# Two attention models in one kernel: both output products as Strassen's, from outputs kept in DRAM

## The chip, the cores and the metric

The kernel runs on one core of a Trainium2 chip. The metric is the device time of one execution in microseconds (us): the median of several runs. A core has five engines that run side by side, each with its own queue of instructions: TensorE (PE, matrix products into PSUM), VectorE (DVE), ScalarE (ACT), GpSimd (POOL) and SyncE (SP), which issues the DMA transfers here. An instruction waits at the head of its queue until the data and buffers it needs are ready, and what stands behind it waits too.

## The reference, cut to what matters

Two independent attention models over 2048 rows of 1024 columns; their outputs are put side by side. Both end in a product with a 1024x1024 matrix wo.

```python
def _A_ref(x, wq, wk, wv, wo, beta):      # 32 heads of 32, 4 segments of 512 rows
    q, k, v = heads(x @ wq), heads(x @ wk), heads(x @ wv)
    for s in range(4):
        p = softmax(q[s] @ k[s].T * scale + mask)
        o[s] = g * (phi(q[s]) @ M / (phi(q[s]) @ z + 1e-6)) + (1 - g) * (p @ v[s])
        M, z = M + phi(k[s]).T @ v[s], z + phi(k[s]).sum(rows)
    return o @ wo

def _B_ref(x, wqkv, w_phi, wo):           # 32 heads of 32
    q, k, v = split(x @ wqkv)
    phi_q = concat(softmax(q @ w_phi), softmax(-q @ w_phi))
    phi_k = concat(softmax(k @ w_phi), softmax(-k @ w_phi))
    kv, z = phi_k.T @ v, phi_k.sum(rows)
    return (phi_q @ kv / (phi_q @ z + 1e-6)) @ wo

return concatenate([A, B], axis=-1)
```

## The kernel before

**Number format.** TensorE multiplies 16-bit floats. Each 32-bit operand is scaled by a bound of its size and split into a high half (a rounded copy, ScalarE) and a low half (what is left, VectorE or GpSimd); one product of two such operands is three products of halves. `halves` records such a split. A product of 128 rows with a 1024x512 piece of weights is thus 8 x 3 = 24 matmuls of 512 columns, and a row block's whole output product 48.

**Strassen's product.** Where it is used, two blocks of 128 rows and the four quarters of the weights are combined into seven forms each, and seven half-depth products of 4 x 3 = 12 matmuls take the place of eight: 84 matmuls for two row blocks in place of 96. The forms of the rows cost four additions and seven splits, the outputs three additions out of PSUM.

**Stages.** First come the first model's attention (32 units of a segment and four heads), which leaves its outputs o in a DRAM tensor `oa_d`; in its course the second model's weights are prepared. Then, for each of eight pairs of row blocks, the second model's keys and values (Strassen's), their two softmaxes (`expo`) and the sums `kva`, `ez` and `za` over the rows. Then the second model's queries: for each of 16 row blocks its projection (Strassen's, by pairs, out of forms kept in `xf_d`), `expo`, multiplication with the sums of the keys (GpSimd), a split into halves `kls`, a transposing DMA into `pt`, and a small product with the sums into the bank `pv`, in two halves of 16 heads.

**The two output products.** The second model's (`project`) is plain: each half of a query block's result is split straight out of `pv` into a tile `ot` (ScalarE the high half, VectorE the low one), and 2 x 24 matmuls of it with wo (`bo`, prepared among the keys by `keep_bo` and kept in `bo_d`) follow within the queries, with one copy on ScalarE and a store for each half. The first model's stands last, as Strassen's: for each of eight pairs (row blocks c and c + 8) two loads from `oa_d`, four combinations (`comb`), seven splits, seven products (`mult`), four copies (`keep`) and three additions (`store`). Its weights are prepared among the queries (`sizes_out`, `weights`).

**What sets the order.** Every instruction is recorded with an engine, a duration, a priority and what it reads and writes (`Graph.op`), and a list scheduler (`Graph.run`) writes them out: at each step the engine that can start first takes, of those that can start then, the instruction with the lowest priority number. Numbers in the table NUDGE shift the priorities a little. PSUM has eight banks, given out by kind (`proj`, `s`, `misc`, `pv`, `kv`). Where the scheduler leaves TensorE without work for more than 0.5 us by its own reckoning and a bank is free, it puts a few matmuls into that bank which nobody reads (`fill`). Tiles with one tag share `bufs` buffers in turn, so an instruction that writes the next tile of a tag waits for the last reader of an earlier one.

Of the kernel before, what the change touches and what calls it, by code (L numbers as in the profile page):

```python
# [45 lines left out]
NUDGE = {0: 820989, 2: 102852, 3: 529656, 4: 266905, 5: 924189, 6: 435410, 9: 911235, 12: 450738, 13: 124130, 14: 669972,  # L46
# [59 lines left out]
class Graph:  # L106
# [12 lines left out]
    def __init__(self, pools):  # L119
        self.ops, self.tags, self.pools, self.opened, self.lines = [], {}, pools, {}, {}  # L120

# [21 lines left out]
    def op(self, eng, dur, fn, r=(), w=(), prio=0, lat=0.0, short=False, port=False, need=(), kb=256):  # L143
# [36 lines left out]
        o.base, o.at = prio, len(self.ops)  # L180
# [3 lines left out]
        o.prio = (prio + nudge(o.at), len(self.ops))  # L184
# [3 lines left out]
    def control(self, fn, opens=()):  # L188
        o = self.op("CTL", 0.0, fn, prio=-1)
        o.deps = [(d, 1) for d in self.ops[:-1]]  # L190
        for pool in opens:
            self.opened[pool] = o

# [114 lines left out]
def tile_kernel(ctx: ExitStack, tc: tile.TileContext, ax, aw, awv, awo, beta, bx, bwqk, bwv, bphi, bwo, out):  # L308
# [10 lines left out]
    wo_d = dram.tile([4, 128, 2, 4, 512], F16, name="wo_d")  # L319
    bo_d = dram.tile([2, 2, 128, 2, 4, 512], F16, name="bo_d")  # L320
# [787 lines left out]
    wfb, xfb, bob = (G.fixed(t) for t in (wf_d, xf_d, bo_d))  # L1108
# [198 lines left out]

# [115 lines left out]
    for p in range(NT // 2):  # L1423
        P = PB + 2 * p
        if p in (1, 2):
            keep_bo(p - 1, P + 0.5)
# [239 lines left out]

    P += 1

    for c in range(NT // 2):
        P += 1
# [141 lines left out]
```

## Time and profile before

| | us |
|---|---|
| three runs | 1667.38, 1667.48, 1668.3 (median 1667.48) |
| span of the profiled execution (its own run's time is not given) | 1665.0 |
| TensorE busy from 0 to 100 us | 95.65 |
| idle of TensorE from 900 to 1000 us | 1.43 |
| idle of TensorE from 1150 to 1200 us | 2.93 |

The span runs from the first instruction to the last of one execution. Busy time of an engine is the time in which one of its instructions ran; the starts of two instructions on one engine can lie closer than the first one's duration. A group's row gives line, engine, operation, tiles (written <- read), shapes and count, then the total and the mean of one in ns, then how long the engine stood idle just before such instructions, and what ended that. A row of the timeline gives start, duration, engine, line, operation and count, with the wait before it in brackets. In rows on a wait, "L619 <- ACT cs L625" says that line 619 waited for ScalarE's instruction of line 625.

### The profile page before, as it was taken

The page shows a single profiled execution, that of the slowest core. Times are in us where ns is not written, and L with a number is a line of the kernel's source. Part 1 is how long each engine was busy: PE and PEld are TensorE (multiplying, and loading weights), DVE is VectorE, ACT ScalarE, POOL GpSimd, SP SyncE. Part 2 cuts the span into 40 slices and gives each one's busy share as a digit, 9 for nine tenths or more (in the row PEclk, how much of TensorE's full clock was granted, in tenths as well). Part 3 has the DMA queues.
Part 4 walks back from the last instruction along what each step waited for, and adds up shares of the span by engine and source line. Part 5 has one row for each costly group of instructions (what it writes and reads, how often), then busy time and mean ns, then how long its engine had stood idle before and what let it go on. Part 6 is the DMA issues. An engine that isn't in the chain of part 4 may idle for free.

```text
span 1665.0 us, 35571 instructions
## 1 busy us (share of the span) xinstructions
PE 1645.5 (99%) x12922; PEld 965.4 (58%) x12922; DVE 1358.1 (82%) x3213; ACT 1111.0 (67%) x2044; POOL 1059.8 (64%) x1393
## 2 busy tenths in 40 slices
PE   8999999999999999999999999999999999999999
PEld 7666667667676666766754444445544444444444
DVE  6999989899897888897877898988997787975441
ACT  8799779868787777777865767645755464454431
POOL 4967577577787886967874454545799897640000
PEclk9999999999999999999999999999999999999999
DMA  7845556768456463756576354276556665853311
GB/s 243 234 138 154 162 154 173 207 197 250 104 160 163 132 181 90 198 189 177 153 205 259 121 199 169 86 256 243 179 151 152 163 183 156 215 151 134 121 57 64
DMA packets 265599, 279.68 MB, mean 168 GB/s; under 512 B 162768, under 2 KB 216016, under 8 KB 256848
## 3 DMA queue, kind: packets, MB, share of 16 engines
q1 hardware_dynamic: 265424, 277.42, 55.9%
q8 instruction: 101, 1.65, 0.4%
q14 instruction: 74, 0.61, 0.1%
HBM read 143.34 MB, written 85.00 MB: 137 GB/s over the span
## 4 chain that ended last, share of the span: by engine, by line
PE 78%; DVE 10%; ACT 4%; POOL 4%; issue 2%; DMA 2%; SPq 0%; DVEq 0%; ACTq 0%; POOLq 0%
PE proj L423 25%; PE proj L619 13%; PE misc L423 9%; PE proj L1720 5%; PE s L1035 4%; PE pv L1071 4%; PE s L942 3%; PE s L619 3%; PE s L1720 2%; PE misc L619 2%; PE pv L1656 1%; PE misc L1216 1%; PE misc L1720 1%; DVE mx L1321 1%; DVE s L948 1%
## 5 line engine op out<-in xcount | busy, mean ns | idle before, releaser
L423 PE MATMUL proj<-S,S 128*128 128x512 f16 (+1 forms) x2304 | 494.1, 343 | 0.7 <-ACT S L450 0.2
L423 PEld LDWEIGHTS <-S 128*128 128x128 f16 x3072 | 288.1, 98 | 160.4 <-issue 0.8
L619 PE MATMUL proj<-S,S 128*128 128x512 f16 x1488 | 342.6, 379 | 6.8 <-ACT cs L625 5.7
L619 PEld LDWEIGHTS <-S 128*128 128x128 f16 x1968 | 187.0, 98 | 220.0 <-issue 7.9
L1048 POOL TENSOR_SCALAR_AFFINE_SELECT ph<-ph 128x256 f16<-128x256 f16 (+1 forms) x448 | 195.0, 459 | 109.5 <-DVE ph L1042 94.5
L1042 DVE SCALAR_TENSOR_TENSOR ph<-s,ph 128x512 f16<-128x512 f32 x320 | 208.7, 684 | 51.7 <-ACT ph L1041 46.0
L948 DVE CUSTOM_DVE_ANT_0 s<-s,causal 128x384 f32<-128x384 f32 (+3 forms) x512 | 241.3, 510 | 7.8 <-PE s L942 5.2
L1041 ACT ACTIVATE ph<-s 128x512 f16<-128x512 f32 x320 | 185.5, 648 | 0.7
L423 PE MATMUL misc<-S,ot 128*128 128x512 f16 x768 | 171.0, 379 | 0.0
L1328 ACT ACTIVATE e<-e,sk 128x256 f32<-128x256 f32 x256 | 114.3, 498 | 62.0 <-DVE e L1325 39.7
L423 PEld LDWEIGHTS <-ot 128*128 128x128 f16 x768 | 73.8, 98 | 88.4
L1039 ACT ACTIVATE s<-s,bdl 128x512 f32<-128x512 f32 x160 | 105.8, 702 | 21.6 <-PE s L1035 21.4
L1039 ACT ACTIVATE s<-s,bd 128x512 f32<-128x512 f32 x160 | 103.1, 690 | 22.4 <-PE s L1035 18.4
L1035 PE MATMUL s<-S 104*128 104x512 f16 (+3 forms) x512 | 113.2, 299 | 0.0
L942 PE MATMUL s<-S 96*128 96x512 f16 (+3 forms) x512 | 112.0, 299 | 0.7 <-DVE dm L995 0.3
L423 PE MATMUL proj<-wv,S 128*128 128x256 f16 x768 | 101.2, 272 | 0.0
L1071 PEld LDWEIGHTS <-ph 128*128 128x128 f16 x2560 | 88.9, 96 | 19.0 <-POOL ph L1048 0.8
L1625 POOL TENSOR_TENSOR e<-e,zb 128x512 f32<-128x512 f32 x64 | 85.0, 1342 | 16.2 <-DVE r L1331 13.2
L1071 PE MATMUL pv<-vl,ph 128*128 128x66 f16 (+1 forms) x2560 | 92.4, 184 | 0.0
L1331 DVE TENSOR_REDUCE r<-e 128x32 f32<-128x1024 f32 x64 | 76.6, 1205 | 12.3 <-ACT e L1328 12.0
L619 PE MATMUL s<-S,S 128*128 128x512 f16 x324 | 78.6, 379 | 0.4 <-DVE S L452 0.4
L948 DVE DVE_READ_ACCUMULATOR2_ANT mt<- 128x1 f32 x512 | 72.1, 141 | 0.0
(375 smaller groups left out, 3300.2 us busy)
## 6 DMA issues: line engine op xcount, KB each, us to landing
S<-h SPq DMA_DIRECT2D x192, 128.0 KB
S<-wf_d SPq DMA_DIRECT2D x21, 1024.0 KB
st<-bwqk SPq DMA_DIRECT2D x56, 256.0 KB
wf_d<-fo SPq DMA_DIRECT2D x48, 256.0 KB
out<-os SPq DMA_DIRECT2D x38, 256.0 KB
wf_d<-oT SPq DMA_DIRECT2D x36, 256.0 KB
S<-xf_d SPq DMA_DIRECT2D x9, 1024.0 KB
S<-aw SPq DMA_DIRECT2D x16, 512.0 KB
```

Source lines behind the costliest of these rows:

```text
L423: op(PE, dur, lambda c=c, a=a, b=b, lv=lv, rv=rv: nc.tensor.matmul(pv(), lv(), rv(), start=(c == 0 and a + b == 0), stop=(c == n - 1 and a ...
L619: op(PE, 0.2165, lambda n=n, a=a, b=b, lv=lv, rv=rv: nc.tensor.matmul(ps(), lv(), rv(), start=(start and n == 0 and a + b == 0), stop=(n = ...
L942: nc.tensor.matmul(ps()[:, o:o + 128 * i + 128], st()[0:96, 0, h, 128 * i:128 * i + 128], st()[0:96, 1, h, 0:128 * i + 128], start=True, s ...
L948: dve({128: 0.216, 256: 0.381, 384: 0.6, 512: 0.648}[n], lambda h=h, i=i, o=o, n=n: nc.vector.tensor_tensor_reduce(ps()[:, o:o + n], ps()[ ...
L1035: nc.tensor.matmul(ps()[:, o:o + n], st()[0:104, 1, h, 128 * j:128 * j + 128], st()[0:104, 0, h, 128 * j:512], start=True, stop=True)
L1039: act(0.571, lambda: nc.scalar.activation(ps(), ps(), AF.Exp, bias=0.0, scale=bd()[:, 4, i2, 0:1]), r=[(bd, i2)], w=[ps])
L1041: act(0.478, lambda: nc.scalar.activation(ph()[:, 0], ps(), AF.Copy, scale=2.0 ** 14), r=[ps], w=[(ph, 0)])
L1042: dve(0.6, lambda: nc.vector.scalar_tensor_tensor(ph()[:, 1], ps(), 2.0 ** 14, ph()[:, 0], op0=OP.mult, op1=OP.subtract), r=[ps, (ph, 0)], ...
L1048: nc.gpsimd.affine_select(pd, pd, pattern=[[0, n], [1, 128]], compare_op=OP.is_ge, fill=0.0, base=0, channel_multiplier=-1)
L1071: nc.tensor.matmul(ps()[:, i, n0:n1], ph()[:, a, o:o + 128], vl()[:, j, h4 + h, n0:n1], start=(i == 0 and a == 0), stop=(j == min(i, 2)), ...
L1328: op(ACT, 0.41, lambda i=i: nc.scalar.activation(e()[:, 4 * i:4 * i + 4], e()[:, 4 * i:4 * i + 4], AF.Exp, bias=0.0, scale=sk()[:, i:i + 1 ...
L1720: op(PE, 0.2165, lambda n=n, a=a, b=b: nc.tensor.matmul(ps(), v(a)[:, n, :], wform[w]()[:, b, n, :], start=(start and n == 0 and a + b == ...
```

## The change

Both output products are Strassen's now, and one function, `outer(o, c, ...)`, records a pair of either: o = 0 is the first model (row blocks c and c + 8, from `oa_d`), o = 1 the second (blocks 2c and 2c + 1, from a new DRAM tensor `ob_d`).

- The first model's pairs move ahead: pair 0 among the last keys, pairs 1 to 7 among the queries of the second model. Its weights are prepared among the keys (pairs 0 to 4), through buffers `zb` and `kls`, and all seven forms are kept in `wo_d`.
- The second model's weights are sized among the keys and formed among the first four queries, on ScalarE and GpSimd; `keep_bo` and its 16 splits on VectorE are gone.
- A query half's result is copied out of `pv` by ScalarE into one buffer, `late[0]` (tag `e5`), sized by a second pass of ScalarE, and stored to `ob_d`; the split of `ot` out of `pv` on VectorE is gone. When both blocks of a pair are done, `sizes_rows` makes the pair's scale: a maximum, one product of one column and three small instructions on VectorE.
- The second model's pairs follow one by one between the later queries, and the last of them ends the kernel.
- A query pair's seven forms come by seven loads of 256 KB in place of two larger ones; the tag `e` has four buffers and a fifth under a tag of its own; `ot` is split in two tags of two.

```diff
@@ tile_kernel
-    wo_d = dram.tile([4, 128, 2, 4, 512], F16, name="wo_d")
-    bo_d = dram.tile([2, 2, 128, 2, 4, 512], F16, name="bo_d")
+    wo_d = dram.tile([2, 7, 128, 2, 4, 512], F16, name="wo_d")
+    ob_d = dram.tile([NT, 128, NG, 128], F32, name="ob_d")
...
+        if p == 0:
+            for j in range(4):
+                sizes_out(0, j, P + 0.5)
+        if p == 3:
+            for j in range(4):
+                sizes_out(1, j, P)
+        if p in (1, 2, 3, 4):
+            weights(0, p - 1, P + 0.5)
...
+    def outer(o, c, rows, P, raw, ss, ring, keeps, kinds, last=False):
...
+        f0, f1 = form(a11), form(a12)
+        comb(s1, a21, a22, OP.add)
+        f3 = form(s1)
+        comb(s3, a11, a21, OP.subtract)
+        comb(s2, s1, a11, OP.subtract)
+        if few:
+            mult(X, f0, 0, True)
+        f2 = form(s2)
+        comb(s4, a12, s2, OP.subtract)
...
+        p1 = keep(X, keeps[0])
+        store(p1, k0, 0, Y)
...
+    own(0, 0, PB + NT - 3, (("b", "zb"), ("b", "kls"), False), ("s", "misc", "s"))
...
+    early(0, 1, P - 2.5)
     for c in range(NT):
-        P = Q0 + c
+        P = Q0 + 3 * c
...
+        if c < 4:
+            weights(1, c, P, False)
+        if c < 6:
+            early(0, c + 2, P + 1.5)
...
-            op(DVE, 0.6, lambda pn=pn, hb=hb, otv=otv: nc.vector.scalar_tensor_tensor(
-                otv()[:, 1, 4 * hb:4 * hb + 4, :], pn(), 2.0 ** -15, otv()[:, 0, 4 * hb:4 * hb + 4, :], op0=OP.mult, op1=OP.subtract),
-               r=[pn, (ot, (0, hb))], w=[(ot, (1, hb))], prio=P)
-        project(lambda a, g: (ot, None, lambda otv=otv: otv()[:, a, g, :]), bo, c * 128, 1024, P + 1.1)
+            op(ACT, 0.478, lambda pn=pn: nc.scalar.activation(
+                late[0]()[:, 0].rearrange("p (g t) -> p g t", t=128), pn(), AF.Copy, scale=2.0 ** -15), r=[pn], w=[(late[0], "pn")], prio=P)
+            op(ACT, 0.614, lambda pn=pn, c=c, hb=hb: nc.scalar.activation(
+                pn(), pn(), AF.Abs, scale=2.0 ** -15, accum_out=obs()[:, 2 * c + hb:2 * c + hb + 1]), w=[pn, (obs, (c, hb))], prio=P)
+            op(SP, 0.6, lambda c=c, hb=hb: nc.sync.dma_start(
+                ob_d[c, :, 4 * hb:4 * hb + 4, :].rearrange("p g t -> p (g t)"), late[0]()[:, 0]),
+               r=[(late[0], "pn")], w=[(obb, (c, hb))], prio=P, lat=1.5, kb=256)
...
     for c in range(NT // 2):
-        P += 1
...
+        sizes_rows(c, Q0 + 6 * c + 7)
...
+    for c in range(NT // 2):
+        last_pairs(c, Q0 + (19.5, 25.5, 31.5, 33.5, 37.5, 43.5, 45.5, 47.5)[c])
```

How the instructions stand now, in three places. The numbers behind the tiles' names tell buffers apart. First VectorE in the middle of the queries. Before, in the eighth query's block: `d1`, `mx`, `dn` and `e` belong to the queries, `ot` is the low half of a result out of `pv`.

```order
L1662 SCALAR_TENSOR_TENSOR ot_19867<-pv_19828,ot_19867 128x512
L1634 RECIPROCAL d1_19874<-d1_19874 128x16
L1321 TENSOR_REDUCE mx_19895<-proj_19759 128x16 x2
L1628 TENSOR_REDUCE dn_19909<-e_19576 128x16
L1323 TENSOR_TENSOR e_19913<-proj_19759,mx_19895 128x16x32
L1325 TENSOR_TENSOR e_19913<-mx_19895,proj_19759 128x16x32
L1634 RECIPROCAL d1_19903<-d1_19903 128x16
L1662 SCALAR_TENSOR_TENSOR ot_19867<-pv_19916,ot_19867 128x512
```

Of the change, at the same stage: L1556 are a pair's combinations, L458 its splits, L1583 its additions out of PSUM, with `ot1` the pair's rows and `ot2` its forms.

```order
L1556 TENSOR_TENSOR ot1_19936<-ot1_19901,ot1_19936 128x512
L458 SCALAR_TENSOR_TENSOR ot2_20471<-ot2_20445,osc3_19186,ot2_20471 128x512
L1346 TENSOR_REDUCE r_20535<-e_20488 128x32
L1583 SCALAR_TENSOR_TENSOR kva_20538<-misc_20483,osc3_19186,kva_20538 128x512
L1347 RECIPROCAL r_20535<-r_20535 128x32
L1556 TENSOR_TENSOR ot2_20445<-ot2_20445,ot1_19901 128x512
L458 SCALAR_TENSOR_TENSOR ot2_20471<-ot1_19936,osc3_19186,ot2_20471 128x512
L635 TENSOR_TENSOR cs_20567<-cs_20567,proj_20116 128x512
```

The split of `ot` is gone, and a pair's combinations, splits and additions stand between the queries' instructions.

Next TensorE where a pair's first product begins. Before, at the end of the queries: `misc` is the last row block's plain product, `proj` the first pair's first product.

```order
L423 MATMUL misc_21628<-S5_17506,ot_21556 128x512
L1720 LDWEIGHTS S15_21174
L1720 MATMUL proj_21672<-S10_18423,S15_21174 128x512
L423 LDWEIGHTS ot_21556
L423 MATMUL misc_21676<-S6_17567,ot_21556 128x512
```

Of the change, at one of the second model's pairs (`s`, out of `ot2`) behind the last projection of queries (`proj`):

```order
L625 LDWEIGHTS S12_17780
L625 MATMUL proj_21527<-S7_18231,S12_17780 128x512
L387 MATMUL fill_22164<-ident_86 128x128 x3
L1569 LDWEIGHTS ot2_22148
L1569 MATMUL s_22168<-S0_20217,ot2_22148 128x512
```

Where a pair's first product had a row block's plain product around it, three filler matmuls stand ahead of it now. From the keys on the order before has three such places, the change's has eight.

Last ScalarE, on the way of a query half's result out of `pv`. Before, in the seventh query's block (`e` are the queries' exponentials, `cs` a form of weights or a partial product, `os` a plain product on its way out):

```order
L529 ACTIVATE cs_19803<-h3_19387 128x512
L1540 ACTIVATE os_19806<-misc_19607,wo2_128 128x512
L1660 ACTIVATE ot_19765<-pv_19775 128x512
L1328 ACTIVATE e_19717<-e_19717,sk_19024 128x256
L625 ACTIVATE cs_19824<-proj_19698 128x512
```

Of the change, near the end of the queries, where two halves follow each other (L1793 the copy, L1795 the size, L456 a pair's split):

```order
L1343 ACTIVATE e_22214<-e_22214,sk_21000 128x256
L1793 ACTIVATE e5_18497<-pv_22296 128x512
L1795 ACTIVATE pv_22296,obs_18603<-pv_22296 128x512
L1793 ACTIVATE e5_18497<-pv_22373 128x512
L456 ACTIVATE S12_22415<-S8_22145,osc3_19186 128x512
L1795 ACTIVATE pv_22373,obs_18603<-pv_22373 128x512
```

Each half takes two instructions in place of one, and the second copy into `e5_18497` stands behind the store of the first.

More of the change, by code (lines that the diff above doesn't have):

```diff
@@ L179, in op @@
         o.deps = [(d, 0) for d in ends] + [(d, 1) for d in starts - ends if d is not o]
-        o.base, o.at = prio, len(self.ops)
+        o.base, o.at = prio, None if free else self.places
+        self.places += not free
         last = self.ops[-1] if self.ops else o
@@ L1532, in zv @@
     def zv():
         return zb().rearrange("p a (two s d) -> p (a two) s d", two=2, s=2)
-    def project(o, w, row, col, prio):
-        for n in range(2):
-            ps = bank("misc", [128, 512])
-            product((ps, ps), o, at(w[n]), NG, prio, dur=0.2168)
-            os = G.buf("stage", [128, 512], F32, "os", 1)
-            op(ACT, 0.587, lambda os=os, ps=ps, n=n: nc.scalar.activation(os(), ps(), AF.Copy, scale=wo2[:, n:n + 1]),
-               r=[ps, wo2b], w=[os], prio=prio)
-            op(SP, 0.6, lambda os=os, n=n: nc.sync.dma_start(
-                out[row:row + 128, col + 512 * n:col + 512 * n + 512], os()), r=[os], prio=prio, lat=1.5)
@@ L1572, in tile_kernel @@
[L1572 to L1589 removed]
+    late.append(G.buf("b", [128, 2, 512], F32, "e5"))
@@ new lines, in tile_kernel, with sizes_rows @@
+    obs, osc3 = G.buf("b", [128, 2 * NT], F32, "obs", 1), G.buf("b", [128, NT // 2, 4], F32, "osc3", 1)
+    def sizes_rows(p, prio):
+        op(DVE, 0.071, lambda: nc.vector.tensor_reduce(osc3()[:, p, 3:4], obs()[:, 4 * p:4 * p + 4], axis=AX.X, op=OP.max),
+           r=[(obs, (c, h)) for c in (2 * p, 2 * p + 1) for h in range(2)], w=[(osc3, (p, 3))], prio=prio)
+        scale(((osc3, (p, 3)), lambda: osc3()[:, p, 3:4]), 1, (osc3, (p, 0), lambda: osc3()[:, p, 0:2]), prio, "misc", 13)
+        op(DVE, 0.1, lambda: nc.vector.tensor_scalar(
+            osc3()[:, p, 2:3], osc3()[:, p, 0:1], wsc[:, 1, 0, 0:1], osc2[:, 1, 0:1], op0=OP.mult, op1=OP.mult),
+           r=[(osc3, (p, 0)), (wscs, (1, 0)), (oscs, 1)], w=[(osc3, (p, 2))], prio=prio)
```

380 lines of the change are left out of this document (193 added, 187 removed), and 33 rows, old and new, of the table NUDGE.

## The prediction

> **What bounds the kernel now.** I read the page's first block, then the table by stretches of time, then the waits of TensorE (PE) from 900 us on, since up to the first key projection (about 905 us) both programs hold the same instructions in the same order.
>
> ```profile
> span 1665.0 us, 35571 instructions
> PE 1645.5 (99%) x12922; PEld 965.4 (58%) x12922; DVE 1358.1 (82%) x3213; ACT 1111.0 (67%) x2044; POOL 1059.8 (64%) x1393
> ```
>
> The columns of the next view are the stretch, its length, then busy time (and instructions) of PE, weight load, VectorE (DVE), ScalarE (ACT), GpSimd (POOL), then the granted clock, the DMA share and GB/s.
>
> ```profile
> 100.00:200.00 100.00, 99.85 (x960) 68.78 (x958) 95.10 (x289) 86.72 (x158) 69.72 (x111) 1.00 0.54 153
> 1200.00:1250.00 50.00, 47.59 (x308) 23.50 (x307) 49.41 (x78) 26.12 (x49) 46.26 (x54) 1.00 0.64 174
> 1250.00:1300.00 50.00, 50.00 (x353) 23.86 (x351) 37.52 (x55) 28.43 (x48) 47.37 (x50) 1.00 0.67 163
> 1300.00:1350.00 50.00, 49.92 (x332) 23.74 (x331) 41.43 (x61) 29.73 (x57) 42.85 (x46) 1.00 0.68 190
> 1350.00:1400.00 50.00, 50.00 (x333) 23.71 (x331) 36.52 (x51) 24.68 (x43) 42.91 (x47) 1.00 0.55 148
> 1400.00:1450.00 50.00, 50.00 (x333) 23.69 (x332) 43.26 (x68) 20.73 (x38) 35.77 (x46) 1.00 0.67 180
> 1450.00:1500.00 50.00, 50.00 (x352) 23.90 (x351) 40.31 (x58) 26.13 (x43) 24.28 (x29) 1.00 0.63 170
> 1550.00:1600.00 50.00, 50.00 (x234) 22.65 (x233) 24.21 (x36) 20.62 (x32) 0.00 (x0) 1.00 0.27 100
> 1600.00:1665.00 65.00, 61.01 (x283) 27.46 (x281) 15.68 (x22) 14.62 (x23) 0.00 (x0) 0.99 0.17 61
> ```
>
> The queries run from about 1200 to 1500, the first model's output pairs after that. PE is never idle for long; in the last row it is idle 4.0 us, which is the eviction and store behind the last matmul. Its longest wait is
>
> ```profile
> PE proj L619 <- ACT cs L625: 5.7, 3, 2.4
> ```
>
> (us in all, times, longest). So time is what PE must issue, plus its few gaps. Busy PE alone could hide slow matmuls, so I take their rate from the chain of waits:
>
> ```profile
> 1246.38 10.36 PE misc L423 x48
> 1117.06 5.18 PE proj L619 x24
> 1220.57 1.46 PE pv L1656 x48
> ```
>
> 48 matmuls of 512 columns in 10.36 us are 0.216 us each, the same in both kinds of product; a query half's 24 small ones take 0.73 us.
>
> **What is removed.** The second model's product (L423, misc<-S,ot) is 768 matmuls; as eight pairs of 7 x 12 it is 672. The first model's 672 stay, only earlier. 96 x 0.216 = **-20.7 us**, all of it on PE.
>
> **What is added on PE.** Each of the second model's pairs gets its own scale: ten such one-column products from the keys on, where there were three. One costs PE the 0.14 us between the first two rows here:
>
> ```profile
> 1211.10 0.28 PE L434 MATMUL s<-ast,one 128*128 128x1 f32 x2
> 1211.24 0.91 PE L381 MATMUL fill<-ident 128*128 128x128 f32 x6
> 1211.99 2.75 PE L619 MATMUL proj<-S,S 128*128 128x512 f16 x12
> 1214.58 0.83 PE L381 MATMUL fill<-ident 128*128 128x128 f32 x6
> 1217.82 2.75 PE L619 MATMUL proj<-S,S 128*128 128x512 f16 x12 [2.41 <-ACT cs L625]
> 1184.05 0.69 PE L381 MATMUL fill<-ident 128*128 128x128 f32 x4
> 1184.58 0.53 PE L1475 MATMUL kv<-ot,pt 128*128 128x65 f16 x12
> ```
>
> 7 x 0.14 = **+1.0 us**.
>
> **New waits of PE.** The program puts filler matmuls where it leaves PE without work. From the keys on there were three such places; the change's order has eight (two in the last keys, five among the queries, one in the pair before the last). The rows above show the three: 0.53 us (1184.05 to 1184.58), 0.75 (1211.24 to 1211.99) and 3.24 (1214.58 to 1217.82, filler and wait), 4.5 in all, 1.5 each. Five more are 5 x 1.5 = **+7.5 us**; with the smallest and the largest +2.7 to +16.2. Nothing in the trace shows a pair waiting for its halves between queries, so I take the mean and keep both ends.
>
> They are plausible because the cover changed. A row's product used to be 96 matmuls that needed one finished ot; a pair's product needs loads, four combinations and seven splits first, and a second-model pair also the row's way out to DRAM and back. Behind the last query's product stand 48 matmuls, 10.4 us; the way to the last pair's first split is two trips through DRAM and three instructions.
>
> ```profile
> ACT kls L1643 <- DMA pt<-kls: 13.2, 3, 9.9
> ```
>
> Waits for a transfer among the queries were 4.4 us on average, so 2 x 4.4 + 0.6 + 0.7 + 0.7 = 10.8, just about the cover, and the eighth filler stands there. I count it in the 7.5 only.
>
> **VectorE.** This decides whether 7.5 is right.
>
> ```profile
> L1662 DVE SCALAR_TENSOR_TENSOR ot<-pv,ot 128x512 f16<-128x512 f32 x30 | 20.2, 675 | 2.0 <-ACT ot L1660 1.8
> L452 DVE SCALAR_TENSOR_TENSOR ot<-e,osc,ot 128x512 f16<-128x512 f32 x12 | 8.6, 748 | 0.0
> L452 DVE SCALAR_TENSOR_TENSOR S<-S,osc,S 128x512 f16<-128x512 f32 x7 | 5.8, 885 | 0.0
> L1687 DVE TENSOR_TENSOR zb<-e 128x512 f32<-128x512 f32 x6 | 4.1, 685 | 0.0
> L1687 DVE TENSOR_TENSOR S<-S,S 128x512 f32<-128x512 f32 x2 | 1.9, 946 | 0.0
> L1687 DVE TENSOR_TENSOR S<-S 128x512 f32<-128x512 f32 x2 | 1.5, 753 | 0.0
> L1569 DVE TENSOR_TENSOR wsc<-wsc,osc 128x1 f32<-128x1 f32 x1 | 1.7, 1722 | 0.0
> L1687 DVE TENSOR_TENSOR kls<-e 128x512 f32<-128x512 f32 x2 | 1.4, 689 | 4.4 <-DMA pt<-kls 4.4
> L1744 DVE SCALAR_TENSOR_TENSOR st<-misc,wsc,st 128x512 f32<-128x512 f32 x7 | 5.3, 751 | 29.7 <-PE misc L1720 29.7
> 1576.33 1.42 DVE L452 SCALAR_TENSOR_TENSOR ot<-e,osc,ot 128x512 f16<-128x512 f32 x2
> ```
>
> Two splits of 748 ns end after 1.42 us, so back to back one takes 0.08 less than its mean. A pair is 4 combinations at 0.60, 7 splits at 0.67 and 3 stores' additions at 0.67: 9.1 us with POOL idle (the rows at 748 and 685), and 4 x 0.87 + 7 x 0.80 + 2.0 = 11.1 us beside a busy POOL (885 and 946). DVE was busy 248.4 us from 1200 to 1500 (its six rows above), in which all 32 query halves' splits lie. The change drops 30 x 0.595 = 17.9 us there (L1662), and the first pair's pieces in these rows were 5.8 + 1.9 + 1.5 + 1.7 + 1.4 = 12.3 us. That leaves 218. Between the change's first and last query product stand 88 splits, so 12.6 pairs: 218 + 115 to 218 + 140, **333 to 358 us**. PE has there 1571 matmuls of 0.216 and 31 halves of 0.73, **362 us**. DVE would stand at 92 to 99%. At 95.1% (100 to 200 us) PE lost 0.15 us of 100; at 98.8% (1200 to 1250) it lost 2.4 of 50. POOL was busy 239 us of those 300 and would spread the same work over 362, so DVE meets it less often: I take the middle, 95 to 96%, where short gaps come but no steady loss. That fits the 7.5.
>
> **Costed at nothing.**
>
> ```profile
> L450 ACT ACTIVATE ot<-e,osc 128x512 f16<-128x512 f32 x14 | 9.4, 714 | 10.9 <-PE misc L1720 7.6 <-DMA e<-oa_d 1.9 <-PE misc L423 1.4
> L1564 ACT ACTIVATE h<-h 128x512 f32<-128x512 f32 x16 | 9.8, 616 | 1.1 <-DMA h<-awo 1.1
> L1540 ACT ACTIVATE os<-misc,wo 128x512 f32<-128x512 f32 x32 | 21.7, 679 | 28.2 <-PE misc L423 20.7 <-DMA out<-os 5.2 <-issue 1.5
> L530 POOL TENSOR_TENSOR cs<-h,cs 128x512 f16<-128x512 f32 x16 | 19.8, 1246 | 9.7 <-ACT cs L529 9.7
> ```
>
> ScalarE was busy 156 us from 1200 to 1500. Among the queries it gets 88 splits at 0.71, some 48 copies at 0.68 and 32 sizes at 0.62, less 32 row copies at 0.68: +93, so 249 of 362 us. PE's matmuls hide that; uncovered it costs up to 93. GpSimd gets 44 combinations and differences among the keys, 44 x 1.25 = 55 us; from 1250 to 1300 it stood at 95% with PE full, so I take zero, and 55 if that cover is gone. The rows' way through DRAM is 32 x 256 KB each way, 17 MB; at a DMA share of 0.68 PE was full too. Behind the last matmul nothing changes.
>
> One wait is new on ScalarE: every half's copy goes through one buffer, e5, and waits for the store before it; exponentials and splits queue behind, and PE waits for these. The nearest row is a product's copy through one buffer, os in the rows above: 5.2 us of waiting over 32 copies, so zero for PE. Were all 32 to wait 3 us, it would be 96 us on an engine with 113 to spare.
>
> **The sum.** -20.7 + 1.0 + 7.5 = -12.2: a span of 1652.8. No time of the profiled execution itself is shown; the runs' median stands 2.5 us above its span, and I keep that distance: 1667.5 - 12.2 = **1655.3 us**.
>
> **Rivals.**
>
> (a) The gain arrives whole: -20.7 + 1.0 = -19.7, **1647.8 us**. For it: PE loses 0.1 us from 1250 to 1500. Against: five more filler places.
>
> (b) DVE runs short all through, as from 1200 to 1250: 2.4 us of each 50 over 362 are 17.4, so -2.3, **1665.2 us**. For it: 99% at the upper price. Against: PE work of other pairs stands in between.
>
> (c) Slower: DVE becomes the bound among the queries, since its instructions with two inputs in SBUF wait for GpSimd's.
>
> ```profile
> L1325 DVE TENSOR_TENSOR e<-mx,proj 128x512 f32<-128x512 f32 x21 | 14.2, 674 | 0.0
> L1325 DVE TENSOR_TENSOR e<-mx,cs 128x512 f32<-128x512 f32 x7 | 8.4, 1199 | 0.0
> ```
>
> The same subtraction takes 674 ns from PSUM and 1199 from SBUF, 0.525 more. If the 140 combinations and splits that stand there pay that, DVE needs 333 + 73.5 = 406.5 us, 44.5 more than PE: 1667.5 - 19.7 + 44.5 = **1692 us**. Below (362 - 333) / 140 = 0.21 us each it costs nothing, above (362 + 19.7 - 333) / 140 = 0.35 the kernel is slower. The rows say 0.14 for a split and 0.26 for a combination, below it; the 1199 row speaks for it. [...]
>
> (d) It doesn't do what it says, since PE is not the path: the three places and the tail are nearly all of PE's idle time after 900 us, so hardly; 1667.5.
>
> **Chances.** Forecast 0.42, (a) 0.27, (b) 0.14, (c) 0.13, the rest 0.04. A range of 1646 to 1671 holds the forecast with both ends of the waits (1650.5 and 1664.0), (a) and (b), 0.83. 0.2% is 3.3 us, about what a measurement can tell from no change: faster 0.75, same 0.11, slower 0.14.
>
> **What would show it.** Right: 96 fewer matmuls of 512 columns, PE idle 4 to 13 us more after 900 us, in gaps of 1 to 3 us ahead of a pair's first matmul or a query's product, released by DVE or ACT; DVE at 92 to 97% among the queries; splits at 0.75 to 0.85 us. Wrong towards (a): gaps no more than before. Wrong towards (b) and (c): DVE above 98% in several stretches, or splits above 1 us. Also wrong: ScalarE idle for the stores of e5 by tens of us, or a gap above 5 us before the last pair.

## The result, and the profile after

The changed kernel took **1679.83 us** (median of four runs, 1678.26 to 1681.51), beside 1667.43 us of the kernel before on the same chip (1665.92 to 1668.3): a ratio of 1.0077, with an interval of 1.0065 to 1.0089. It is slower by 12.4 us, where 12.2 us less were forecast. The profiled execution's span is 1676.9 us, 11.9 more than before.

First the head of the page, and of its chain of waits the shares by engine.

```profile
span 1676.9 us, 36137 instructions
PE 1636.2 (98%) x12874; PEld 958.6 (57%) x12874; DVE 1454.6 (87%) x3305; ACT 1179.2 (70%) x2200; POOL 1130.6 (67%) x1437
PE 61%; DVE 24%; ACT 7%; issue 3%; DMA 2%; POOL 2%; SPq 0%; DVEq 0%; ACTq 0%; POOLq 0%
```

TensorE has 48 matmuls fewer (96 products less, fillers and scales more) and 9.3 us less busy time, so the change did remove work. But VectorE is busy 96 us more, and its share of the chain, 10% before, is 24%. The stretches of the queries show where (columns as in the prediction).

```profile
1250.00:1300.00 50.00, 48.91 (x286) 22.25 (x284) 44.93 (x59) 32.63 (x62) 38.29 (x36) 1.00 0.82 233
1300.00:1350.00 50.00, 47.37 (x260) 21.62 (x259) 42.31 (x54) 31.39 (x55) 39.87 (x39) 1.00 0.71 214
1350.00:1400.00 50.00, 48.07 (x281) 21.66 (x280) 47.89 (x66) 28.48 (x54) 39.60 (x40) 1.00 0.78 219
1400.00:1450.00 50.00, 47.85 (x285) 22.55 (x284) 49.93 (x76) 25.54 (x48) 30.16 (x35) 1.00 1.08 290
1450.00:1500.00 50.00, 49.25 (x353) 24.29 (x351) 40.09 (x61) 27.65 (x53) 23.22 (x24) 1.00 0.65 171
1500.00:1550.00 50.00, 48.30 (x302) 22.08 (x300) 48.94 (x76) 29.17 (x59) 25.68 (x34) 1.00 0.74 175
1550.00:1600.00 50.00, 45.78 (x312) 21.39 (x311) 49.30 (x74) 29.80 (x56) 30.19 (x32) 1.00 0.50 135
1248.00:1643.00 395.00, 377.75 (x2373) 176.10 (x2373) 362.58 (x512) 229.56 (x428) 246.41 (x257) 1.00 0.73 198
```

Before, TensorE was full in nearly all of these rows; now no row is, and VectorE (the third number behind the comma) stands at 98 to 100% in three of them. A full VectorE is not the whole story, though: from 1300 to 1350 us it is busy for 85% only, and TensorE is 2.6 us short there as well. The last row covers the stretch from the first to the last small product `pv` of a query half: VectorE has 362.58 us of work in 395, TensorE by the prediction's count 362.

The idle time of TensorE understates the loss, since a matmul's recorded end lies later than the start of the next (a mean of 0.379 us is recorded for one of 512 columns, where one starts every 0.216 us), so I also compare stages from the start of their first product to the end of their last. These are the first and the last `pv` of the change in the timeline (before, the first started at 1220.50 and the last ended at 1501.83):

```profile
1248.22 0.86 PE L1789 MATMUL pv<-pt,st 128*64 128x128 f16 x24
...
1642.61 0.86 PE L1789 MATMUL pv<-pt,st 128*64 128x128 f16 x24
```

The stretch takes 395.2 us, 33 more than its 362 of matmuls (28 fillers, 3.9 us, are among the 33). From the first to the last product `kv` of the keys it is 295.3 us, where before had 275.6; by counting the matmuls in both, 8.3 of these 19.7 us are work (the first pair) and 11.4 are new stalls. From the last `kv` to the first `pv` some 6 us of stalls are gone.

What TensorE waited for, the five largest rows of the whole run:

```profile
PE s L1569 <- DVE ot L458: 7.2, 10, 2.0
PE s L1569 <- ACT ot L456: 4.7, 7, 1.3
PE kv L1526 <- DVE pt L1519: 4.2, 6, 1.0
PE s L1569 <- ACT kls L456: 2.3, 1, 2.3
PE misc L1569 <- DVE ot L458: 2.2, 3, 1.3
```

Four of the five rows are a pair's product (L1569) waiting for a pair's splits, and the third is the keys'. L458 is VectorE's low half, L456 ScalarE's high one, and ScalarE, by its row on the page, had stood idle for VectorE's combinations (L1556) most of the time before it:

```profile
L456 ACT ACTIVATE ot<-ot,osc 128x512 f16<-128x512 f32 x68 | 47.6, 715 | 49.0 <-DVE ot L1556 41.8
```

So what is late is VectorE's. The groups of VectorE in the query stretch, different shapes apart:

```profile
L458 DVE SCALAR_TENSOR_TENSOR ot<-ot,osc,ot 128x512 f16<-128x512 f32 x52 | 53.0, 1036 | 2.5 <-ACT ot L456 2.5
L1556 DVE TENSOR_TENSOR ot<-ot,ot 128x512 f32<-128x512 f32 x23 | 26.7, 1166 | 0.0
```

The same instructions had 748 and 685 ns where nothing disturbed them before. All 87 splits of that stretch average 0.96 us and all 50 combinations 1.12. A piece of the timeline, VectorE and GpSimd together, shows what they do in that time:

```profile
1316.61 2.35 POOL L1770 TENSOR_TENSOR e<-e,r 128x1024 f32<-128x1024 f32 x1
1317.12 2.39 DVE L458 SCALAR_TENSOR_TENSOR ot<-ot,osc,ot 128x512 f16<-128x512 f32 x1
1319.43 0.68 DVE L1556 TENSOR_TENSOR ot<-ot,ot 128x512 f32<-128x512 f32 x1
1320.92 0.61 PE L1569 MATMUL s<-S,ot 128*128 128x512 f16 x2 [1.34 <-ACT ot L456]
1321.16 0.74 DVE L458 SCALAR_TENSOR_TENSOR ot<-ot,osc,ot 128x512 f16<-128x512 f32 x1
```

The split at 1317.12 starts while GpSimd multiplies by `r` and ends 0.55 us after it; with GpSimd idle, the next combination takes 0.68 and the next split 0.74. Then TensorE waits 1.34 us for that pair. A wait of this kind stands inside the instruction's duration (2.39 us recorded), so the profile calls VectorE busy.

The 0.55 us is no chance. Of the 137 splits and combinations of the stretch, 54 start while GpSimd runs one of its two large products or an instruction on weights, and 49 of these end 0.545 to 0.553 us after that instruction does, with anything from 0.2 to 1.9 us of it left at their start (of the other five, four start in its last 0.11 us). The remaining 83, beside an idle GpSimd or a small instruction of 16 or 32 columns, average 0.73 us (splits) and 0.68 us (combinations). So what these instructions wait for is the end of the GpSimd instruction that runs when they start.

### The profile page after: what moved, and what is told of

Same layout as the page of the kernel before. It is cut to its first block, busy times and chain, and to the rows that moved or that the text cites. A ratio compares the mean times of both kernels' runs of the same rounds, so it can differ in the third digit from the quotient of the medians.

```text
span 1676.9 us, 36137 instructions
## 1 busy us (share of the span) xinstructions
PE 1636.2 (98%) x12874; PEld 958.6 (57%) x12874; DVE 1454.6 (87%) x3305; ACT 1179.2 (70%) x2200; POOL 1130.6 (67%) x1437
## 4 chain that ended last, share of the span: by engine, by line
PE 61%; DVE 24%; ACT 7%; issue 3%; DMA 2%; POOL 2%; SPq 0%; DVEq 0%; ACTq 0%; POOLq 0%
PE proj L429 25%; PE proj L625 8%; PE s L1569 7%; PE s L1041 3%; PE s L948 3%; PE pv L1077 3%; DVE mx L1336 3%; DVE ot L458 2%; DVE r L1346 2%; DVE ot L1556 2%; PE s L625 1%; DVE e L1340 1%; DVE e L1338 1%; PE misc L1569 1%; DVE kls L1778 1%
## 5 line engine op out<-in xcount | busy, mean ns | idle before, releaser
L625 PE MATMUL proj<-S,S 128*128 128x512 f16 x1500 | 356.7, 379 | 1.3 <-ACT pq L631 0.9
L1569 PE MATMUL s<-S,ot 128*128 128x512 f16 x876 | 205.5, 379 | 13.4 <-DVE ot L458 7.2
L1569 PEld LDWEIGHTS <-ot 128*128 128x128 f16 x1056 | 99.6, 98 | 144.7 <-DVE ot L458 19.8
L1758 POOL TENSOR_TENSOR e<-e,zb 128x512 f32<-128x512 f32 x64 | 93.3, 1472 | 59.1 <-DVE r L1346 43.3
L456 ACT ACTIVATE ot<-ot,osc 128x512 f16<-128x512 f32 x68 | 47.6, 715 | 49.0 <-DVE ot L1556 41.8
```

The costliest lines, as they stand in the source:

```text
L625: op(PE, 0.2165, lambda n=n, a=a, b=b, lv=lv, rv=rv: nc.tensor.matmul(ps(), lv(), rv(), start=(start and n == 0 and a + b == 0), stop=(n = ...
L1569: op(PE, 0.2165, lambda n=n, a=a, b=b: nc.tensor.matmul(ps(), t[2](a)[:, n, :], w[f]()[:, b, n, :], start=(start and n == 0 and a + b == 0 ...
```

## The experiments

Four theories were told apart. A: VectorE's instructions with two inputs in SBUF wait for GpSimd's reads. B: the pairs' loads, the way through DRAM and the single buffers set the waits. C: GpSimd's own chain of instructions for a query half is late. D: VectorE's load as such is the bound. For the keys, K1 puts the new stalls down to GpSimd's work on weights, K2 to ScalarE, the first pair or the order. Each ratio is to the kernel before, measured beside the run (1666.4 to 1666.8 us). The changed kernel is taken at 1679.8, when the kernel before stood at 1667.4, so a difference from it is good to about 1 us. Except in one experiment (combinations on GpSimd) every instruction stands at the place that it has in the changed kernel, or in the kernel before for the last one.

### GpSimd's reads taken away

```diff
-nc.gpsimd.tensor_tensor(e()[:, 8*a:8*a+8], e()[:, 8*a:8*a+8], zv()[:, h0:h0+8], op=OP.mult)
+[nc.gpsimd.memset(e()[:, 8*a:8*a+8], 0.03) for _ in range(2)]
...
-nc.gpsimd.tensor_tensor(e(), e(), bc32(r), op=OP.mult)
+[nc.gpsimd.memset(e(), 0.03) for _ in range(2)]
```

> The changed kernel with every instruction at its place, but GpSimd's two large multiplications of each query half (by zb, 512 columns, and by r, 1024 columns, both reading SBUF) are replaced by fills of the same tile that read nothing, two in a row so that GpSimd is busy about as long (1.1 and 1.9 us in place of 1.48 and 2.01). The queries' probabilities are then a constant. Theory A (VectorE bounds the queries because its instructions with two inputs in SBUF wait for GpSimd's reads): between the first and last small query product the splits fall from a mean of 0.96 to 0.75 us, the combinations from 1.12 to 0.69 us, VectorE's busy time by some 35 to 40 us, and the time by 15 to 25 us, to 1655 to 1665. Theory B (the pairs' loads, the trip through DRAM and the single buffers set the waits, VectorE's load does not matter): the instructions may get shorter but the time stays within 5 us of 1679.8. Theory C (GpSimd's own chain of seven instructions per query half is what is late): the fills are 15% shorter, so 2 to 6 us less.

Measured: 1659.18 us (ratio to before 0.9953, 0.9938 to 0.9968), 20.6 less than the changed kernel. The same groups of VectorE and the same piece of the timeline, now with fills:

```profile
L458 DVE SCALAR_TENSOR_TENSOR ot<-ot,osc,ot 128x512 f16<-128x512 f32 x52 | 41.3, 809 | 4.8 <-ACT ot L456 3.0 <-PE s L1569 1.6
L1556 DVE TENSOR_TENSOR ot<-ot,ot 128x512 f32<-128x512 f32 x23 | 17.7, 775 | 0.0
```

```profile
1315.42 1.95 POOL L1769 MEMSET e<- 128x1024 f32 x2
1315.95 0.74 DVE L458 SCALAR_TENSOR_TENSOR ot<-ot,osc,ot 128x512 f16<-128x512 f32 x1
1316.61 0.68 DVE L1556 TENSOR_TENSOR ot<-ot,ot 128x512 f32<-128x512 f32 x1
```

The split that took 2.39 us takes 0.74 beside a GpSimd that is busy at the same place. The waits of TensorE among the queries nearly vanish:

```profile
PE s L1569 <- DVE ot L458: 0.9, 3, 0.4
PE s L1569 <- ACT ot L456: 0.5, 1, 0.5
```

The stretch from the first to the last `pv` is 375.0 us, 20.2 shorter; the keys stay at 295.7 (295.3 in the changed kernel). A is borne out and B falls: the transfers were not touched.

In all, the fills were shorter than what they replaced (GpSimd was busy 210 us in the row from 1248 to 1643, in place of 246), so theory C had to be excluded:

```diff
-[nc.gpsimd.memset(e()[:, 8*a:8*a+8], 0.03) for _ in range(2)]
+[nc.gpsimd.memset(e()[:, 8*a:8*a+8], 0.03) for _ in range(3)]
...
+nc.gpsimd.memset(e()[:, 0:3], 0.03)
```

> As with the fills in place of GpSimd's two multiplications (e1_memset, 1659.2), but each now as long as or longer than the multiplication was in the changed kernel: three fills of 512 columns (1.57 us, the multiplication had 1.48 on average, 1.27 when nothing held it up) and two of 1024 with one of 192 (2.1 us, against 2.01). The queries' probabilities are a constant. Theory A (what costs is VectorE's two-input instructions waiting for GpSimd's reads): 1657 to 1664, splits and combinations as short as in e1_memset. Theory C (what cost was GpSimd's own chain, which the fills of 1.05 us shortened): at least 1672.

Measured: 1661.44 us (0.9969, 0.9958 to 0.9981). GpSimd was busy 252 us in the row from 1248 to 1643, more than the 246 of the changed kernel, and it cost 2.3 us. So it is not GpSimd's time. It is what the fills leave out, its reads; that they leave out the arithmetic too, no run here separates.

### VectorE's combinations cut to almost nothing

```diff
-nc.vector.tensor_tensor(to[2](), a[2](), b[2](), op=f)
+nc.vector.tensor_tensor(to[2]()[:, :, 0:2], a[2]()[:, :, 0:2], b[2]()[:, :, 0:2], op=f)
...
-f5 = form(s4)
+f5 = form(s4, a12)     # splits a12; likewise f3 splits a21, f2 and f4 split a11
```

> The changed kernel with every instruction at its place, but the four combinations of each pair work on 8 columns of 512, and the splits behind them read the quarters themselves. It leaves out the sums and differences of the row blocks. VectorE loses 60 instructions of about 1.0 us each, some 50 of them between the first and last small query product: 362.6 us there become about 312 of 395. Theory A (VectorE is the bound among the queries): stalls of 29.8 us there fall to 5 to 10 and the time to 1655 to 1662. Theory B (loads, DRAM and single buffers): each pair's way is 4 us shorter, but the waits for transfers stay; 1672 to 1680. If VectorE's two-input instructions wait for GpSimd, the splits that are left still take 0.9 us or more.

Measured: 1673.74 us (1.0038, 1.0023 to 1.0053), 6 less, as B had it, and far from A's 1655 to 1662. And together with the fills:

> e1_memset and e2_comb8 together: fills in place of GpSimd's multiplications, and combinations of 8 columns, order unchanged. The queries' probabilities are a constant, and the row blocks' sums and differences are left out. VectorE then has some 285 of the 365 us in which TensorE works among the queries. If VectorE's load as such is a bound (theory D), taking off its 50 combinations counts here as well: 1650 to 1655. If only the waits for GpSimd counted (theory A), the combinations cost nothing once these are gone: 1657 to 1660, as in e1_memset.

Measured: 1666.63 us (1.0001, 0.9992 to 1.0011), 7.4 *more* than with the fills alone, outside both bounds. Less work on VectorE could not do that, and the trace of this run shows a wait that the changed kernel does not have, and in SyncE's queue one that has grown:

```profile
PE pv L1789 <- DMA pt<-kls: 5.6, 3, 2.4
```

```profile
SPq L1551 <- DVE ot L458: 36.9, 10, 8.8
```

A load for the next pair (L1551) waited in SyncE's queue for a split, 36.9 us in all. In the changed kernel the same loads waited 9.3 us for splits and 14.9 for combinations, at most 5.4 at a time. The transposing transfers stood behind it. This was my edit: the split of the last difference now read the first two quarters' buffer, which so came free later. Mended:

```diff
-f5 = form(s4, a12)
+f5 = form(s4, a22)     # f2 splits a22 too, f4 a21
```

> Again combinations of 8 columns (e2_comb8), with one thing mended: there the split of the last difference read the first two quarters' buffer, which so came free later, and SyncE's load for the next pair waited up to 8.8 us for it with the transposing transfers queued behind. Now the splits behind the combinations read quarters of the other buffer, and the order is that of the changed kernel. It leaves out the sums and differences of the row blocks. Theory A (VectorE's waits for GpSimd's reads are what costs): the combinations still wait for GpSimd although they have nothing to do, 0.4 us and more each, so only a part of 20.6 us is won: 1666 to 1674. Theory D (VectorE's load as such is the bound): 1656 to 1662.

Measured: 1664.47 us (0.9986, 0.9976 to 0.9995), 15.4 less than the changed kernel, between the bounds that I gave A and D. In its trace none of TensorE's larger waits is for a transfer. With the fills:

> The mended combinations of 8 columns together with the fills of e1_memset. Left out: the queries' probabilities, the row blocks' sums and differences. Theory A: without GpSimd's reads the combinations cost the kernel nothing, so the time of e1_memset, 1657 to 1661, without the 6 us that e8_both lost to transfers. Theory D: 1650 to 1655.

Measured: 1655.98 us (0.9933, 0.9918 to 0.9948). This too lies between the bounds. These four kernels belong in one table (us; in brackets VectorE's busy share of each kernel's own stretch from the first to the last `pv`):

| | GpSimd reads | GpSimd fills |
|---|---|---|
| combinations whole | 1679.8 (92%) | 1659.2 (85%) |
| combinations of 8 columns | 1664.5 (88%) | 1656.0 (79%) |

The combinations cost 15.4 us beside reads and 3.2 without them; the reads cost 20.6 beside whole combinations and 8.5 beside cut ones. So most of either cost arises only together with the other, as if VectorE had room for the pairs' work or for the waits and not for both. The table does not show that it is room alone: both edits also shorten each pair's way to its splits. D alone is not it, since 50 combinations less bring just 3.2 us when the waits are gone, and A as I had put it is not all of it either, since the waits that remain cost less once VectorE has room. The group of the cut combinations shows the wait itself, first beside reads, then beside fills:

```profile
L1556 DVE TENSOR_TENSOR ot<-ot,ot 128x8 f32<-128x8 f32 x23 | 11.2, 494 | 0.0
```

```profile
L1556 DVE TENSOR_TENSOR ot<-ot,ot 128x8 f32<-128x8 f32 x23 | 5.7, 253 | 0.4 <-ACT ot L456 0.4
L1556 DVE TENSOR_TENSOR h<-h,h 128x8 f32<-128x8 f32 x4 | 0.6, 162 | 0.8 <-ACT ot L456 0.7
```

An addition of 8 columns takes 0.16 us undisturbed and 0.49 on average beside reads: it waits although it has almost nothing to do. Of the 30 cut combinations that start, beside reads, while GpSimd runs an instruction, 28 end 0.016 to 0.027 us after that instruction does. (With fills some still meet GpSimd's work on weights, hence 0.25.)

### GpSimd among the keys

```diff
-nc.gpsimd.tensor_tensor(pv(), av(), bv(), op=o)
+nc.gpsimd.tensor_tensor(pv()[:, 0:8], av()[:, 0:8], bv()[:, 0:8], op=o)     # o == 0
...
-nc.gpsimd.tensor_tensor(lv(), pv(), hv(), op=OP.subtract)
+nc.gpsimd.memset(lv(), 0.001)                                                # o == 0
```

> The changed kernel with every instruction at its place, but GpSimd's 44 combinations and differences for the first model's weights among the keys are cut down: the combinations work on 8 columns, the differences are replaced by fills that read nothing. The first model's weights are then not right. GpSimd gets some 45 us less between the first and last key, and nothing else changes. Theory K1 (these instructions, in the way of the keys' own on GpSimd and in the way of VectorE, make the 11 us of new stalls among the keys): 1667 to 1673. Theory K2 (ScalarE's sizes and scalings, the first pair at the end of the keys, or the order alone make them): 1676 to 1682. The queries' part stays as it is in both.

Measured: 1674.01 us (1.004, 1.0026 to 1.0054), 5.8 less. The stretch from the first to the last `kv` is 289.5 us in place of 295.3, and TensorE's wait for `pt`, 4.2 us in the changed kernel, is 1.2:

```profile
PE s L1571 <- ACT kls L456: 2.3, 1, 2.3
PE s L1571 <- DVE kls L458: 1.5, 2, 0.9
PE kv L1528 <- DVE pt L1521: 1.2, 2, 0.9
```

K1 explains 5.8 of the 11.4 us; of the rest, 3.8 are the first pair's splits (`kls`), which these rows show unchanged. What is left, some 2 us, no run settles. Nor does this run tell which part of K1 it is: it takes away GpSimd's reads and 40 of its 206 us of work among the keys at once, so VectorE's waits and GpSimd's own delay fall together. Then both places at once:

> The fills among the queries (e1_memset, 20.6 us less) and the cut down weights of the first model among the keys (e3_keys8, 5.8 less) together. Left out: the queries' probabilities and the first model's weights. If both are the same thing, GpSimd's reads in VectorE's way at two places that don't touch each other, the gains add up: 1652 to 1656, which is where the change was forecast with GpSimd's part at nothing. If one only moves the wait to the other: 1657 to 1662.

Measured: 1652.21 us (0.9912, 0.9897 to 0.9927), 27.6 less than the changed kernel, where the two alone give 20.6 + 5.8 = 26.4. The two places don't touch each other.

### The kernel before, with the fills

> The kernel before with the same fills in place of GpSimd's two multiplications of each query half; all else at its place. The queries' probabilities are a constant. Among its queries VectorE has few instructions with two inputs in SBUF (32 differences of 1024 columns, 7 subtractions, some splits of the first pair), so theory A has it at 1663 to 1667, at most 4 us less; if GpSimd's reads were in the way there as well, the 20 us that they cost the changed kernel would not be the change's: 1655 or below.

Measured: 1663.17 us (0.9976, 0.9965 to 0.9986), 3.6 less. Its stretch from the first to the last `pv` is 281.2 us with the fills and 281.3 without: among its queries GpSimd's reads cost the kernel before nothing. Three of the 3.6 us lie between the last `kv` and the first `pv` (32.4 us in place of 35.4), where the first pair's splits stand.

### Ways out that did not work

The combinations on GpSimd, planned anew:

```diff
-op(DVE, 0.6, lambda: nc.vector.tensor_tensor(to[2](), a[2](), b[2](), op=f),
+op(POOL, 1.23, lambda: nc.gpsimd.tensor_tensor(to[2](), a[2](), b[2](), op=f),
```

> The changed kernel with the pairs' 60 combinations on GpSimd (1.25 us each), the order planned anew. It computes all of the reference. VectorE loses some 52 us of its 362.6 between the first and last small query product, GpSimd gains 60 to 65 on 246 of 395. Theory A (VectorE's time is the bound): 1662 to 1672, since the splits meet GpSimd more often (mean 1.0 us or above). Theory B (the length of a pair's way from its load to its splits): four instructions get 0.2 to 0.6 us longer each, so 1679 to 1690.

Measured: 1696.84 us (1.018, 1.0163 to 1.0197), far from A's 1662 to 1672 and above B's. The group of splits and the row of the query stretch:

```profile
L458 DVE SCALAR_TENSOR_TENSOR ot<-ot,osc,ot 128x512 f16<-128x512 f32 x52 | 57.9, 1132 | 16.4 <-ACT ot L456 12.3 <-PE s L1569 3.7 <-PE misc L1569 0.3
```

```profile
1248.00:1643.00 395.00, 384.44 (x2417) 191.06 (x2416) 316.76 (x457) 222.03 (x413) 305.51 (x299) 1.00 0.69 192
```

The row covers only a part of this kernel's stretch. Over the whole of it, from 1237 to 1660 us, VectorE has 332 us of work, 30 less than in the changed kernel, and GpSimd 323 in place of 246. VectorE's splits get longer still (1.13 us), and a pair's way to its splits leads through GpSimd's queue, so that TensorE got 304 fillers where the changed kernel has 76, and the stretch of the queries took 423.5 us.

GpSimd's instructions cut into smaller ones, so that VectorE has less to wait out:

```diff
-nc.gpsimd.tensor_tensor(e(), e(), bc32(r), op=OP.mult)
+[nc.gpsimd.tensor_tensor(e()[:, i:i+8], e()[:, i:i+8], bc32(r)[:, i:i+8], op=OP.mult) for i in (0, 8)]
```

> The changed kernel with GpSimd's multiplication by r (1024 columns, 2.01 us) as two instructions of 512 columns, all else at its place. It computes all of the reference. If a VectorE instruction waits out the GpSimd instruction that runs when it starts (theory A), its wait behind this line falls from up to 1.9 us to up to 1.0, so combinations from 1.12 to about 1.0 and splits from 0.96 to about 0.93; GpSimd pays about 0.1 to 0.2 us more per query half, and the time falls by 2 to 8 us, to 1672 to 1678. If the two share the path word by word, cutting changes nothing but GpSimd's overhead: 1679 to 1683.

> The changed kernel with GpSimd's multiplication by r as four instructions of 256 columns and that by zb as two of 256, all else at its place. It computes all of the reference. Theory A: waits of up to 0.6 us in place of 1.3 and 1.9, splits at 0.85 and combinations at 0.85 to 0.9 us, but GpSimd's chain for a query half gets some 0.8 us longer: 1668 to 1677. If GpSimd's own chain is what is late (theory C), 1682 to 1690.

Measured: 1681.63 us (1.0089, 1.0074 to 1.0104) and 1681.03 us (1.0088, 1.0073 to 1.0103), no better than the changed kernel. Both miss A's bounds, and the first falls within those of a path shared word by word. That reading is out all the same: a combination of 8 columns, 0.16 us alone, took up to 1.88 us beside reads (run e9_comb8b). In the second:

```profile
L1556 DVE TENSOR_TENSOR ot<-ot,ot 128x512 f32<-128x512 f32 x23 | 23.3, 1021 | 0.0
```

```profile
1248.00:1643.00 395.00, 379.91 (x2356) 176.04 (x2355) 352.86 (x513) 230.50 (x427) 291.62 (x409) 0.99 0.72 197
```

The waits did get shorter (a combination 1.02 us in place of 1.17, a split 0.99 in place of 1.04), though not to the 0.85 to 0.9 that I had expected. GpSimd is busy 45 us more, so more instructions meet it. VectorE got 9.7 us back, and the time nothing; why not even a part of it is open.

## Why the prediction was wrong

**What was removed and added on TensorE** was right: 96 products less, seven scales more. With GpSimd's reads away at both places the changed kernel takes 1652.2 us, near the forecast of 1655.3. Of the 12.4 us that it lost, 20.6 - 3.6 = 17.0 are GpSimd's reads among the queries over what they cost the kernel before, and 5.8 its work on weights among the keys. Without these, 12.4 - 17.0 - 5.8 = -10.4 us would stand where -12.2 was forecast. So 19.7 - 10.4 = 9.3 us of new waits are left beside my 7.5, but that the two are near is in part luck. Among the queries 13 us were left and among the keys 5.6, more than twice the 7.5, and the 6 us that went between the keys and the queries set off a part of it.

**The step that failed** is the one on VectorE, "4 x 0.87 + 7 x 0.80 + 2.0 = 11.1 us beside a busy POOL", and "DVE meets it less often: I take the middle, 95 to 96%, where short gaps come but no steady loss". The prices of a disturbed split and combination came from the rows at 885 and 946 ns, and these are means over instructions most of which met nothing. The first pair before stood between 1457 and 1483 us, where GpSimd was at work for only 24 of 50 us, and its timeline holds the full price:

```profile
1475.14 1.72 POOL L1625 TENSOR_TENSOR e<-e,zb 128x512 f32<-128x512 f32 x1
1475.65 2.42 DVE L452 SCALAR_TENSOR_TENSOR S<-S,osc,S 128x512 f16<-128x512 f32 x2
```

The first of these two splits takes 1.76 us and ends 0.55 us after the product with `zb`; the other six of the seven take 0.74, and the mean is 0.885. So the mean held how seldom a split met GpSimd's large products there, and that did not carry over: among the queries of the changed kernel 54 of 137 met one, or an instruction on weights. Measured means were 0.96 and 1.12 us: over the quiet rows 0.21 for each of 87 splits and 0.43 for each of 50 combinations, where I had 0.14 and 0.26. On average that is 0.29, in the middle between my 0.21, below which nothing was to be lost, and 0.35, above which the kernel was to be slower. What such an instruction pays depends on which instruction of GpSimd it meets, and how much of that is left. Of those that stand singly in the timeline of the query stretch, by what GpSimd ran at their start (mean us, count):

| GpSimd runs | splits | combinations |
|---|---|---|
| nothing | 0.73 (25) | 0.68 (17) |
| a small one (16 or 32 columns) | 0.74 (16) | 0.70 (6) |
| work on weights (512 columns), 1.2 to 1.5 us | 1.09 (6) | 1.10 (5) |
| the product with `zb`, 1.48 us | 1.43 (12) | 1.53 (9) |
| the product with `r`, 2.01 us | 1.60 (4) | 2.16 (7) |
| the same two as fills (first fill run) | 0.73 and 0.74 (13, 5) | 0.67 and 0.68 (10, 10) |

I should have priced the wait from the length of GpSimd's instructions and their share of the time (146 us of the two large ones in 395), not from a mean over a stretch with another mixture.

**The bounds of 0.21 and 0.35 us** failed with it. VectorE's work came to 362.6 us, only 4.6 above my upper end of 358 and level with TensorE's 362, so by my rule it should still have cost next to nothing. The rule spread VectorE's work evenly. But three of the stretches above are full, and a single wait stopped TensorE, for 1.34 us, where VectorE was not full: the split of 2.39 us stands in the row from 1300 to 1350, at 85%, on the way from a combination through ScalarE's split to a pair's product. So 7.5 us of new waits became 33 us over the matmuls of the query stretch. With the fills 13 remained there, and with the cut combinations besides 11, at 79% of VectorE; what those are, beyond the 28 fillers, no run settles.

**GpSimd among the keys**, costed at nothing with 55 us as the other end: its work on weights cost 5.8 us, and all in all the keys lost 11.4.

**The rivals.** What happened is (c), VectorE as the bound through waits for GpSimd, in a size between (b) with 1665.2 and (c) with 1692. It had a chance of 0.13, and two of the signs named for it came: VectorE above 98% in several stretches (two, and a third at 97.9%), and splits above 1 us in the largest group. I had set (c) aside on the strength of the rows at 885 and 946 ns. The runs bear out the wait that it supposes: a split with both inputs in SBUF waited out GpSimd's product with `r` (2.39 us in place of 0.74), combinations of 8 columns waited too (0.49 us in place of 0.16), and splits that met the fills did not wait (0.73 and 0.74 us). Nor did those with one input in SBUF that the stretch has: the 60 sums `dn<-e`, 31 of which started beside a large product or work on weights, took 0.668 us on average in the changed kernel and 0.673 with the fills, the 21 subtractions `e<-mx,proj`, whose other input is in PSUM, 0.671 and 0.674.

**ScalarE, the way through DRAM, `e5`, the last pair** were right to be costed at nothing: in the changed kernel TensorE's waits among the queries name no transfer, and ScalarE nearly always with splits of a pair (0.2 us are another), which by its row had mostly waited for a combination themselves. The edit that held a pair's buffer longer shows how near that was: SyncE's queue, blocked for up to 8.8 us, cost 1673.74 - 1664.47 = 9.3 us.

## What to carry to other kernels

Before moving work to an engine that is "82% busy", ask with what operands the new instructions come: an addition or a split of 512 columns with both inputs in SBUF took its own time here beside an idle GpSimd (0.68 and 0.73 us). Beside one of GpSimd's large products or its work on weights it took what was left of that instruction and some 0.55 us, up to 2.48 us, and the profile booked the wait as busy time. Price it from the other engine's instruction lengths in the stretch to which the work moves, and single out the instructions that met it: a mean over a row hides them. Nor is a mean load of VectorE enough to judge its room, since TensorE lost time in full stretches and, on the way to a pair, at 85% too. To test such a suspicion, replace the reads by fills of the same length, and compare the same instruction in both timelines.

## What the runs showed of the hardware that was not expected

Behind two waits of TensorE the granted clock fell. In the run of e8_both, TensorE waited 2.35 and 1.32 us for transposing transfers between 1490 and 1495 us, with two matmuls between; the windows of 4 us around it (columns as in the prediction; the granted clock stands third from the end):

```profile
1488.00:1492.00 4.00, 2.60 (x13) 1.08 (x11) 2.50 (x4) 0.00 (x0) 0.00 (x0) 1.00 0.77 182
1492.00:1496.00 4.00, 1.73 (x25) 1.37 (x25) 0.00 (x0) 2.33 (x5) 0.00 (x0) 0.62 1.10 341
1496.00:1500.00 4.00, 4.00 (x11) 1.40 (x12) 3.76 (x4) 3.40 (x8) 0.21 (x1) 0.52 1.12 291
1500.00:1504.00 4.00, 4.00 (x20) 1.84 (x19) 3.71 (x8) 2.46 (x5) 1.83 (x4) 1.00 1.29 242
```

From 1496 to 1500 TensorE is never idle and gets through 11 matmuls at a clock of 0.52, where the next window has 20: the gap cost about 2 us a second time, after it had ended (12 matmuls from 1495.91 to 1500.42, 4.5 us, where 12 x 0.216 are 2.6). The run of e2_comb8 has waits of 2.23 and 1.35 us at the same place, up to 1497, and a clock of 0.50 from 1496 to 1500 and 0.66 from 1500 to 1504. From what length of a pause on the clock falls was not shown: no run here varies it. In the changed kernel itself no wait among the queries was above 2.0 us, and its clock in the rows above stayed at 1.00.

And GpSimd's fills, at 0.52 us for 512 columns, did not disturb VectorE (0.73 and 0.74 us for a split beside fills, 0.73 beside an idle GpSimd), while the product with `zb` that reads the same tile, at 1.27 us or more, did (1.43 us for a split).
